# Front of a fused attention and feed-forward kernel: seven sets of six transposes, undivided exponentials, a buffer for each block of words, and second weights loaded by ScalarE

## The chip, the cores and the metric

The kernel runs on one core of a Trainium2 chip. The metric is the device time of one execution in microseconds, and less is better. The core has a matrix engine (TensorE, PE in the rows), VectorE (DVE), ScalarE (ACT), GpSimd (POOL) and a queue engine SyncE (SP) that mostly issues DMA transfers. Each engine works through its own list of instructions in order and waits on semaphores where it needs another's result.

## The reference

```python
w = softmax(weight_gen, axis=-1)            # (4, 4096, 8, 7), float32
x_unf = causal window of 7 rows of x        # x: (4, 4096, 192)
att[b,s,h,g] = sum_k w[b,s,h,k] * x_unf[b,s,k,h,g]     # 8 heads of 24
h = att.reshape(16384, 192) @ w_in          # (192, 2048), float64
g = max(0.01 * h, h)
out = float32(g @ w_out)                    # (2048, 192), float64
```

The inputs w_in and w_out have eight bytes a number; the kernel reads them as pairs of 32-bit words and makes float32 numbers and then two float16 halves of them.

## The kernel before

The 16384 tokens lie on 128 partitions with 128 rows each. A chunk is 4 rows, 512 tokens, and there are 32 chunks. A chunk's attention output is made by thirteen operations on GpSimd (`conv_ops`: one product, then six times product and sum). It is scaled by a power of two per token, split into two float16 halves (`split_h` on ScalarE, `split_l` on GpSimd), transposed by VectorE in blocks (`squares`), written to DRAM (`put_squares`, tile `far`) and read back transposed (`get_squares`, tile `xx`). TensorE then makes for each pair of 128 features the product with w_in (`mm1`, tile `hp`), ScalarE the leaky maximum (`leak`) and the upper half, VectorE the lower half (`gl`), and TensorE the product with w_out (tiles `po`).

The first chunk is another matter, since nothing is loaded or split yet when it starts. Its attention output is made by VectorE and GpSimd together, GpSimd for the last 12 of the 32 groups of a row and head. The sums over the 7 taps are partly left to TensorE: each set of taps is multiplied into a tile `parts`, and TensorE transposes the sets one after the other with `is_transpose`, adding them up in PSUM (`add_transposed`, tile `ta`). Copies then bring the sums to SBUF (`first_tokens`, tile `xw`). Its products run in float32: `mm1(0)` to `mm1(7)`, called product 0 to 7 below, each of six matmuls of 512 columns, and sixteen second products (`mm2_whole`) of four matmuls each.

All of this is written out by hand in the string `START`, a letter for a step. Those which matter here:

- `d`, `g`: the next multiplication (or addition) of a set on VectorE, on GpSimd; `t`: the transposes of the next set; `T`: `first_tokens`; `f`: the next product with its two leaks (`leak_out`) on ScalarE; `e`: the next second product.
- `r`: `read_words`, two ScalarE operations on the next of 16 blocks of words (tiles `rnd` and `mag`); `W` or `w`, `o`: VectorE (or GpSimd) makes float32 numbers of them (`widen`, `round_up`, tile `bits`); `m`: `block_max`, the largest magnitude of a block (tile `most`).
- `1`, `2`, `3`: the scales of the weights. `1` takes the maximum over all 16 block maxima (tile `both`) and has TensorE transpose it into `spares`; VectorE reduces that to `top`, `2` has TensorE spread it, and `3` makes the scales. The float16 halves of the weights come behind it.
- `a`, `b`: softmax of the second half of the first piece of weights; `p`: a GpSimd step of the second chunk's attention; `M`, `N`, `E`, `D`: softmax of the second piece; `B`, `C`, `V`, `y`, `Y`, `X`, `R`: scaling, splitting, transposing, writing and reading back of the second chunk.

Words of w_in come in blocks of 2 x 192 KB (three buffers), those of w_out in blocks of 384 KB (two buffers); all of them are loaded by SyncE, and each `read_words` call asks for a later block. From the second chunk on a loop runs `step(q)` for each pair of features.

Of the kernel before, what the change touches and what calls it, by code (L numbers as in the profile page):

```python
# [8 lines left out]
F32 = mybir.dt.float32  # L9
# [37 lines left out]
SETS = ((6,), (5,), (4, 3), (2,), (1, 0))  # L47
# [19 lines left out]
def conv_attention_moe_kernel(  # L67
# [54 lines left out]
    def load_words(key, eng=nc.sync):  # L122
        q, kind = key
        if kind == IN:
            w = raw.tile([P, NB, P, 2], U32, tag="wi", name="wi_raw", bufs=3)
            for u, r in enumerate(HALVES):
                f = 2 * q + u
                eng.dma_start(out=w[r], in_=w_in_words[:, :, f * P:(f + 1) * P, :])
        else:
            w = raw.tile([P, 2, D, 2], U32, tag="wo", name="wo_raw")  # L130
            eng.dma_start(out=w, in_=w_out_words[:, 2 * q:2 * q + 2, :, :])
        words[key] = w
# [4 lines left out]
    def read_words(key):  # L137
# [3 lines left out]
        nc.scalar.activation(out=rnd, in_=w[:, :, 0], func=AF.Copy, scale=2.0 ** -29)  # L141
        nc.scalar.activation(
            out=mag, in_=w[:, :, 1].bitcast(F32), func=AF.Prelu, scale=REBIAS, alpha=SIGN
        )
        vals[key] = rnd, mag.bitcast(U32)
# [221 lines left out]
    W = J * D + HP  # L367

    def tiles_of_sets():

        tiles = [
            xtp.tile([P, NK, 2, NB, P], F32, tag="parts", name="parts"),
            xtp.tile([P, 2, J, D], F32, tag="sq", name="parts"),
            xtp.tile([P, 2, J, D], F32, tag="split", name="parts"),
        ]
        a, b, c = tiles
        a = a.rearrange("p k i b t -> p (k i b t)")
        b, c = (t.rearrange("p i j d -> p (i j d)") for t in (b, c))
        return [b[:, 0:W], c[:, 0:W], a[:, 0:W], a[:, W:2 * W], a[:, 2 * W:3 * W]]

    def conv_sets(eng, s, w, tmp=None):

        n = s.stop - s.start
        for i, ks in enumerate(SETS):
            dst = parts[i][:, 0:J * D].rearrange("p (h g) -> p h g", g=G)[:, s, :]
            for k in ks:
                out = dst
                if k != ks[0]:
                    t = conv.tile([P, J * D], F32, tag="tmp", name="tmp") if tmp is None else tmp
                    out = t[:, 0:n * G].rearrange("p (h g) -> p h g", g=G)  # L390
                wk = w[:, s, k:k + 1].to_broadcast([P, n, G])
                eng.tensor_tensor(out=out, in0=tap(0, k)[:, s, :], in1=wk, op=ALU.mult)  # L392
                yield
                if k != ks[0]:
                    eng.tensor_tensor(out=dst, in0=dst, in1=out, op=ALU.add)  # L395
                    yield


# [17 lines left out]
    def add_transposed(i):  # L416
# [8 lines left out]
        for b in range(NB):  # L425
            for j in range(J):
                a = (j * NB + b) * HP
                nc.tensor.matmul(
                    out=sums[b][:, j * P:(j + 1) * P], lhsT=v[:, a:a + P],
                    rhs=ident, is_transpose=True, start=(i == 0 and j == 0),  # L430
                    stop=(i == len(SETS) - 1 and j == J - 1), skip_group_check=True,
                )

    def first_tokens():
# [5 lines left out]
        for b in range(NB):  # L440
            h, t = xx[0][:, :, 0, b, :], sums[b].rearrange("p (j t) -> p j t", j=J)
            if b == 0:
                nc.scalar.copy(out=h, in_=t)
            elif b == 1:
                nc.vector.tensor_copy(h, t)
            else:
                nc.scalar.copy(out=h[lo], in_=t[lo])
                nc.vector.tensor_copy(h[hi, 1:J], t[hi, 0:J - 1])
                nc.vector.tensor_copy(h[hi, 0:1], t[hi, J - 1:J])
# [3 lines left out]
    def scale_tokens(c):  # L453

        m = win.tile([P, J, 2], F32, tag="xm", name="xm")[:, :, 0]
# [3 lines left out]
        nc.vector.tensor_reduce(  # L459
            out=m, in_=att[c], axis=AX.X, op=ALU.max, apply_absolute_value=True  # L460
        )
# [3 lines left out]
        nc.gpsimd.tensor_tensor(  # L465
            out=att[c], in0=att[c], in1=up.bitcast(F32).to_broadcast([P, J, D]), op=ALU.mult
        )
# [41 lines left out]
    def mm1(q):  # L509
# [3 lines left out]
        for b in range(NB):  # L513
            b_of = (b, (b + 1) % NB) if c == 0 else (b, b)
            if c < WHOLE:
                w = value((i, IN))
                passes.append(([w[:, k] for k in b_of], xx[c][:, :, 0, b, :]))
                continue
            h, l = xx[c][:, :, 0, b, :], xx[c][:, :, 1, b, :]
            w_h, w_l = ([w[:, i, k] for k in b_of] for w in (wi_h, wi_l))  # L520
# [3 lines left out]
        for m, (w, r) in enumerate(passes):  # L524
            for u, s in enumerate(HALVES):
                nc.tensor.matmul(  # L526
                    out=hp[2 * q + u], lhsT=w[u][s], rhs=r[s],
# [86 lines left out]
    def mm2_whole(ns):  # L614

        for n in ns:
            f = n % NF
            for j in range(J):
                nc.tensor.matmul(  # L619
                    out=po0[j // 2][:, j % 2 * D:(j % 2 + 1) * D],  # L620
                    lhsT=g_h[n][:, j * P:(j + 1) * P], rhs=value((f // 2, OUT))[:, f % 2],
# [82 lines left out]
    def prepare(stage):  # L704
# [9 lines left out]
        if s == "r" and done[s] + 4 <= len(order):  # L714
            load_words(order[done[s] + 3])

    with tc.manual_schedule():
# [44 lines left out]
        def step(q):  # L762
# [18 lines left out]
            else:  # L781
                split_g(2 * q)
                if c == WHOLE and i == TURNS[c][1] + 1:
# [15 lines left out]
            if c + 1 < NCH:  # L799
# [6 lines left out]
                if i == turned:  # L806
                    squares(c + 1, 0)
                    if c != WHOLE:
# [151 lines left out]
```

## Time and profile before

| | us |
|---|---|
| median of 3 runs (lowest, highest) | 1032.48 (1032.46, 1033.61) |
| the profiled execution, its own time | 1032.44 |
| its span, first to last instruction | 1030.7 |
| TensorE busy | 1024.9 |
| GpSimd, ScalarE, VectorE busy | 805.7, 660.2, 566.0 |

The span is what the profile shows in detail; 1.7 us of the profiled execution's time lie around it. Busy time is the time in which an engine had an instruction in work. The page also gives the granted clock of TensorE in forty slices, and it is at its full level in all of them.

### The profile page before, as it was taken

Reading aid. Unit: us, or ns where it says so; the run is one execution under the profiler, and the core shown is the slowest. Engines: PE = TensorE matmul, PEld = TensorE weight load, DVE = VectorE, ACT = ScalarE, POOL = GpSimd, SP = SyncE. Lnnn points to the kernel's source line nnn. Section 1 sums busy time; section 2 is a strip of 40 time slices with the busy share of each in tenths; the row PEclk is TensorE's granted clock in tenths of the full one; section 3 lists DMA queues with packets and bytes.
Section 4 is the critical chain, followed back from the end, with each engine's and each line's share of the span. In section 5 each row is a group of like instructions: output and inputs, shape, how many; then the busy total and the mean of one; then the engine's idle time right before and its main releaser. Section 6 shows DMA issues by size and latency. Waiting matters only on the chain.

```text
span 1030.7 us, 30286 instructions
## 1 busy us (share of the span) xinstructions
PE 1024.9 (99%) x12828; PEld 618.9 (60%) x12828; DVE 566.0 (55%) x1030; ACT 660.2 (64%) x1266; POOL 805.7 (78%) x518
## 2 busy tenths in 40 slices
PE   9999999999999999999999999999999999999998
PEld 7755555565565655555555555565555655656566
DVE  8986555555545555455555555545456454555443
ACT  6576666666666666666666566666666666666664
POOL 7999897777887777987777977778977779977600
PEclk9999999999999999999999999999999999999999
DMA  9432312213223031322213123132320323220120
GB/s 250 147 100 63 126 48 63 95 47 125 55 85 97 32 110 63 110 63 61 94 50 126 48 63 106 36 126 62 94 80 34 109 62 110 63 63 32 48 63 17
DMA packets 42662, 83.08 MB, mean 81 GB/s; under 512 B 4511, under 2 KB 36127, under 8 KB 40734
## 3 DMA queue, kind: packets, MB, share of 16 engines
q1 hardware_dynamic: 42382, 81.05, 25.9%
q8 instruction: 100, 1.64, 0.7%
q14 instruction: 36, 0.29, 0.1%
q10 hardware_dynamic: 144, 0.10, 0.0%
HBM read 56.36 MB, written 24.77 MB: 79 GB/s over the span
## 4 chain that ended last, share of the span: by engine, by line
PE 97%; DMA 1%; POOL 1%; DVE 1%; ACT 0%; issue 0%; SPq 0%; DVEq 0%; POOLq 0%
PE hp L526 49%; PE po L579 47%; PE po L619 1%; DMA xx<-far 0%; POOL parts L392 0%; DVE sq L484 0%; DMA far<-sq 0%; DMA wt<-in_weight_gen_dram 0%; POOL parts L395 0%; POOL tmp L392 0%; DVE gl L550 0%; SPq L501 0%; ACT wt L324 0%; DVE gh L549 0%; ACT hp L532 0%
## 5 line engine op out<-in xcount | busy, mean ns | idle before, releaser
L550 DVE TENSOR_TENSOR gl<-hp,gh 128x512 f16<-128x512 f32 x496 | 335.9, 687 | 345.3 <-ACT gh L547 344.1
L579 PE MATMUL po<-wo,gh 64*128 64x384 f16 (+1 forms) x4096 | 506.5, 318 | 0.0
L579 PE MATMUL po<-wo,gl 64*128 64x192 f16 x3968 | 486.4, 243 | 0.4 <-DVE gl L550 0.3
L532 ACT ACTIVATE hp<-hp 128x512 f32<-128x512 f32 x496 | 292.3, 589 | 274.2 <-PE hp L526 274.1
L526 PE MATMUL hp<-xx,wi_h 64*128 64x512 f16 x2976 | 443.3, 376 | 0.4 <-DMA xx<-far 0.4
L364 POOL TENSOR_TENSOR acc<-acc,tmp 128x768 f32<-128x768 f32 x186 | 336.5, 1809 | 14.6
L547 ACT CAST gh<-hp 128x512 f16<-128x512 f32 x495 | 290.7, 587 | 15.8 <-PE po L579 1.3
L360 POOL TENSOR_TENSOR tmp<-xt,wt 128x768 f32<-128x768 f32 x186 | 287.8, 1547 | 10.0
L526 PE MATMUL hp<-xx,wi_l 64*128 64x512 f16 x1488 | 282.8, 376 | 0.0
L579 PEld LDWEIGHTS <-gh 64*128 64x128 f16 x4096 | 198.4, 94 | 138.9
L526 PEld LDWEIGHTS <-wi_h 64*128 64x128 f16 x2976 | 141.3, 94 | 135.0 <-DMA xx<-far 1.1
L579 PEld LDWEIGHTS <-gl 64*128 64x128 f16 x3968 | 193.0, 94 | 29.8 <-DVE gl L550 1.3
L465 POOL TENSOR_TENSOR acc<-acc,xu 128x768 f32<-128x768 f32 x31 | 45.5, 1469 | 137.2 <-DVE xu L202 137.2
L526 PEld LDWEIGHTS <-wi_l 64*128 64x128 f16 x1488 | 72.7, 94 | 88.2
L484 DVE STREAM_TRANSPOSE sq<-split 128x384 f16<-128x384 f16 x124 | 63.8, 554 | 51.0 <-POOL split L475 50.6
L662 DVE SCALAR_TENSOR_TENSOR ot<-po,xr,ot 128x192 f32<-128x192 f32 x120 | 41.8, 411 | 47.9 <-ACT ot L658 47.9
L471 ACT CAST split<-acc 128x768 f16<-128x768 f32 x31 | 25.8, 832 | 51.0 <-POOL acc L465 51.0
L475 POOL TENSOR_TENSOR split<-acc,split 128x768 f16<-128x768 f32 x31 | 50.9, 1642 | 1.9 <-ACT split L471 1.9
L360 POOL TENSOR_TENSOR acc<-xt,wt 128x768 f32<-128x768 f32 x31 | 48.1, 1552 | 0.2
L658 ACT ACTIVATE ot<-po,xr 128x192 f32<-128x192 f32 x120 | 40.7, 422 | 0.0
L459 DVE TENSOR_REDUCE xm<-acc 128x4 f32<-128x768 f32 x31 | 29.2, 943 | 2.4 <-POOL acc L364 2.4
L619 PE MATMUL po<-bits,g 128*128 128x192 f32 x128 | 22.3, 330 | 0.0
(85 smaller groups left out, 289.7 us busy)
## 6 DMA issues: line engine op xcount, KB each, us to landing
xx<-far SPq DMA_DIRECT2D x124, 192.0 KB, 3.7
xt<-in_x_dram SPq DMA_DIRECT2D x14, 1344.0 KB, 5.8
far<-sq SPq DMA_DIRECT2D x31, 384.0 KB, 2.3
out_dram<-ot SPq DMA_DIRECT2D x62, 192.0 KB, 1.9
wt<-in_weight_gen_dram SPq DMA_DIRECT2D x15, 224.0 KB, 2.6
wi_raw<-in_moe_w_in_dram SPq DMA_DIRECT2D x16, 192.0 KB, 6.2
wo_raw<-in_moe_w_out_dram SPq DMA_DIRECT2D x8, 384.0 KB, 5.4
xt<-in_x_dram SPq DMA_DIRECT2D x2, 384.0 KB, 4.2
```

What stands on the lines that cost most here:

```text
L360: eng.tensor_tensor(out=out, in0=tap(c, k), in1=wk, op=ALU.mult)
L364: eng.tensor_tensor(out=acc, in0=acc, in1=out, op=ALU.add)
L465: nc.gpsimd.tensor_tensor(out=att[c], in0=att[c], in1=up.bitcast(F32).to_broadcast([P, J, D]), op=ALU.mult)
L475: eng.tensor_tensor(out=l, in0=att.pop(c), in1=h, op=ALU.subtract)
L484: nc.vector.transpose(out=sq[c][:, v, i], in_=src[:, v])
L526: nc.tensor.matmul(out=hp[2 * q + u], lhsT=w[u][s], rhs=r[s], start=(m == 0), stop=(m == len(passes) - 1),)
L532: return nc.scalar.activation(out=hp[n], in_=hp[n], func=AF.Prelu, alpha=0.01, scale=DOWN).ins
L547: nc.scalar.copy(out=h, in_=t)
L550: nc.vector.tensor_tensor(out=l, in0=t, in1=h, op=ALU.subtract)
L579: ins = nc.tensor.matmul(out=po[j][:, 0:b - a], lhsT=g[n][s, j * P:(j + 1) * P], rhs=wo[s, f, a:b], start=(f == 0 and i < HALF and m == 0) ...
L658: nc.scalar.activation(out=ot[:, j], in_=po[k * HALF + j][:, D:2 * D], func=AF.Copy, scale=rx[j])
L662: nc.vector.scalar_tensor_tensor(out=ot[:, j], in0=po[k * HALF + j][:, 0:D], scalar=rx[j], in1=ot[:, j], op0=ALU.mult, op1=ALU.add,)
```

## The change

The sets of taps become seven, one for each tap, so that no additions stand on VectorE or GpSimd; each set is transposed in six blocks of 128 columns instead of twelve overlapping ones, which drops the small ScalarE copy ahead of each set. The sums of the six blocks lie in two PSUM tiles, and `first_tokens` copies them to places of their own by eight copies, four on ScalarE and four on VectorE; `first_rows` says where each product finds its halves, and `POS` in which order the second product takes the tokens.

The second half of the first piece keeps its exponentials undivided; the sums are taken by `s` and their reciprocals go into the scaling of the second chunk (`by_head`). Each block of words has a buffer of its own, so SyncE asks for all of w_in at once in step `A`, with the second piece's weights and rows behind it. ScalarE asks for the first four blocks of w_out behind its first exponential (`<`) and for one more at each `z`. `read_words` does `mag` before `rnd`. Last, `squares(c + 1, 1)` of the later chunks moves one step later.

```diff
-SETS = ((6,), (5,), (4, 3), (2,), (1, 0))
+TURNED = (0, 3, 1, 4, 2, 5)
+POS = (0, 2, 1, 3)
 START = (
-    "ZASgdddgtggddtddrgdggtdggrttaWwoTbrrpWrpWf"
-    "rWmppf"
-    "rWrWmpf"
-    "rWmrWmmKppeeeerWmprWmkppf"
-    "rWmrWmMppf"
-    "rWmrWmpWmpNeeeef"
-    "EBCVmmmmf"
-    "e1De2eyY3Xevvhhllevvhhlle"
-    "RvvhhllfvvhhllqqHL"
+    "ZA<Sgdgdtgdtgdrtgdtagdtgdttwbo"
+    "TcrpmWp"
+    "rmfW"
+    "rpWmzrfWm"
+    "rpWmzrsf"
+    "WmzrpWmpeeeerWmf"
+    "rpWmzrWmMppf"
+    "rWmrWmpppprWmNeeeef"
+    "BErWmrWmCVmf"
+    "1eDe2eyY3XevvhhlleRvvhhllevvhhllfvvhhllqqHL"
 )
-            w = raw.tile([P, NB, P, 2], U32, tag="wi", name="wi_raw", bufs=3)
+            w = raw.tile([P, NB, P, 2], U32, tag="wi", name="wi_raw", bufs=NQ)
...
+            w = raw.tile([P, 2, D, 2], U32, tag="wo", name="wo_raw", bufs=NQ)
...
-        v = parts[i]
-        nc.scalar.copy(out=v[:, J * D:W], in_=v[:, 0:HP])
-        for b in range(NB):
-            for j in range(J):
-                a = (j * NB + b) * HP
-                nc.tensor.matmul(
...
+        for n, m in enumerate(TURNED):
+            nc.tensor.matmul(
+                out=sums[n // J][:, n % J * P:(n % J + 1) * P],
+                lhsT=parts[i][:, m * P:(m + 1) * P], rhs=ident, is_transpose=True,
...
+        act(out=x[:, 1:3], in_=a)
+        dve(x[lo, 3], a[hi, 1])
+        dve(x[hi, 0], a[lo, 0])
+        act(out=x[:, 5], in_=b)
+        dve(x[lo, 0], a[hi, 0])
+        dve(x[hi, 3], b[lo])
+        act(out=x[hi, 4], in_=a[lo, 1])
+        act(out=x[lo, 4], in_=b[hi])
...
-                if c == WHOLE and i == TURNS[c][1] + 1:
+                if c + 1 < NCH and i == TURNS.get(c, (1, 3))[1] + 1:
                     squares(c + 1, 1)
...
-        if s == "r" and done[s] + 4 <= len(order):
-            load_words(order[done[s] + 3])
...
+            elif what == "<":
+                for q in range(NQ // 2):
+                    load_words((q, OUT), nc.scalar)
+            elif what == "z":
+                load_words((NQ // 2 + sent, OUT), nc.scalar)
+                sent += 1
```

How instructions stand is shown at three places. The first is ScalarE around the leaks of product 5, the first `g<-hp` row of each piece. `rnd` and `mag` are the two halves of `read_words`, `wt<-wt` the exponential of the second piece, `split` the upper half of the second chunk. Before:

```order
L141 ACTIVATE rnd<-wo_raw 128x384
L142 ACTIVATE mag<-wo_raw 128x384
L141 ACTIVATE rnd<-wo_raw 128x384
L142 ACTIVATE mag<-wo_raw 128x384
L537 ACTIVATE g<-hp 128x512 x2
L324 ACTIVATE wt<-wt 128x448
L471 CAST split<-acc 128x768
L537 ACTIVATE g<-hp 128x512 x2
```

and now:

```order
L557 ACTIVATE g<-hp 128x512 x2
L327 ACTIVATE wt<-wt 128x448
L144 ACTIVATE mag<-wo_raw 128x384
L147 ACTIVATE rnd<-wo_raw 128x384
L144 ACTIVATE mag<-wo_raw 128x384
L147 ACTIVATE rnd<-wo_raw 128x384
L493 CAST split<-acc 128x768
L557 ACTIVATE g<-hp 128x512 x2
```

The last two blocks of words were read ahead of the leaks of product 5 and are now read behind them and behind the exponential.

The second place is TensorE from products 5 and 6 (the row of twelve matmuls into `hp`) to the two steps of the scales (`spares`); a second product is four matmuls into `po`. Before:

```order
L526 MATMUL hp<-xw,bits 128x512 x12
L619 MATMUL po_114<-bits,g 128x192 x2
L619 MATMUL po_115<-bits,g 128x192 x2
L215 MATMUL spares<-ident,both 1x128 x2
L619 MATMUL po_114<-bits,g 128x192 x2
L619 MATMUL po_115<-bits,g 128x192 x2
L223 MATMUL spares<-top,ones 128x2
```

and now:

```order
L546 MATMUL hp<-xw,bits 128x512 x12
L218 MATMUL spares<-ident,both 1x128 x2
L639 MATMUL po_114<-bits,g 128x192 x2
L639 MATMUL po_115<-bits,g 128x192 x2
L639 MATMUL po_114<-bits,g 128x192 x2
L639 MATMUL po_115<-bits,g 128x192 x2
L226 MATMUL spares<-top,ones 128x2
```

The transposes of `both` stood behind one second product and now stand right behind product 6.

The third place is VectorE from its first multiplication of the first chunk (`parts<-xt,po_114`) to the copies of the first tokens (`xw<-ta`). `mx<-wt` is the maximum over the second half of the weights, which needs the second load of `wt`. Before:

```order
L392 TENSOR_TENSOR parts<-xt,po_114 128x480 x3
L392 TENSOR_TENSOR spares<-xt,po_114 128x480
L395 TENSOR_TENSOR parts<-parts,spares 128x480
L392 TENSOR_TENSOR parts<-xt,po_114 128x480 x2
L392 TENSOR_TENSOR spares<-xt,po_114 128x480
L395 TENSOR_TENSOR parts<-parts,spares 128x480
L316 TENSOR_REDUCE mx<-wt 128x32
L152 TENSOR_SCALAR po_115<-mag 128x384
```

and now:

```order
L386 TENSOR_TENSOR parts<-xt,po_114 128x480 x5
L319 TENSOR_REDUCE mx<-wt 128x32
L386 TENSOR_TENSOR parts<-xt,po_114 128x480 x2
L155 TENSOR_SCALAR bits<-mag 128x384
L434 COPY xw<-ta 64x256
L435 COPY xw<-ta 64x256
L437 COPY xw<-ta 64x256
L438 COPY xw<-ta 64x256
```

The maximum stood behind all multiplications and now stands ahead of the last two.

## Rows read from the trace of the kernel before

**Rows 1.** The page's first part: busy time, share of the span, instructions.

```profile
PE 1024.9 (99%) x12828; PEld 618.9 (60%) x12828; DVE 566.0 (55%) x1030; ACT 660.2 (64%) x1266; POOL 805.7 (78%) x518
```

**Rows 2.** Waits of PE: who for whom, total us, times, longest.

```profile
PE hp L526 <- DMA xx<-far: 0.4, 1, 0.4
PE po L579 <- DVE gl L550: 0.3, 1, 0.3
```

**Rows 3.** Timeline of PE: start, length, instruction, count, idle before and its end.

```profile
6.75 6.74 PE L428 MATMUL ta<-ident,parts 128*128 128x128 f32 x60
13.58 8.00 PE L526 MATMUL hp<-xw,bits 64*128 64x512 f32 x36
...
43.00 1.57 PE L619 MATMUL po<-bits,g 128*128 128x192 f32 x8
44.40 0.38 PE L215 MATMUL spares<-ident,both 128*1 128x128 f32 x2
...
54.40 0.38 PE L526 MATMUL hp<-xx,wi_h 64*128 64x512 f16 x1
55.14 0.60 PE L526 MATMUL hp<-xx,wi_h 64*128 64x512 f16 x3 [0.36 <-DMA xx<-far]
```

**Rows 4.** Line 428 on PE: length min/median/max in ns, first and last start.

```profile
L428 PE MATMUL ta<-ident,parts x60: 272/273/298, 6.8 to 13.2; 128*128 128x128 f32 x60
```

**Rows 5.** Timeline of DVE and ACT, 6 to 15 us.

```profile
6.32 1.22 DVE L392 TENSOR_TENSOR parts<-xt,po 128x480 f32<-128x480 f32 x2 [0.16 <-DMA xt<-in_x_dram]
...
11.11 0.38 DVE L316 TENSOR_REDUCE mx<-wt 128x32 f32<-128x224 f32 x1
...
12.66 0.39 ACT L324 ACTIVATE wt<-wt 128x224 f32<-128x224 f32 x1 [1.01 <-POOL wt L319]
...
12.96 0.57 ACT L443 COPY xw<-ta 128x512 f32<-128x512 f32 x1
...
14.14 0.56 DVE L448 COPY xw<-ta 64x384 f32<-64x384 f32 x1 [0.36 <-ACT xw L447]
```

**Rows 6.** Line 284, second load of `wt`: its issue, and us to landing.

```profile
L284 SPq DMA_DIRECT2D wt<-in_weight_gen_dram x1: 598/598/598, 4.7 to 4.7; - x1
...
DMA to landing us min/median/max: 3.7/3.7/3.7
```

**Rows 7.** Busy time by stretch; last three: granted PE clock, DMA share, GB/s.

```profile
1.00:2.00 1.00, 0.54 (x1) 0.50 (x2) 0.54 (x3) 1.00 (x1) 0.29 (x1) 1.00 0.14 25
...
5.00:9.00 4.00, 4.00 (x26) 3.46 (x25) 3.73 (x8) 1.33 (x4) 3.57 (x6) 1.00 1.10 261
```

**Rows 8.** Timeline of ACT, 36 to 42 us.

```profile
36.30 0.54 ACT L142 ACTIVATE mag<-wo_raw 128x384 f32<-128x384 f32 x1
40.52 1.09 ACT L537 ACTIVATE g<-hp 128x512 f32<-128x512 f32 x2 [3.68 <-PE hp L526]
41.50 0.58 ACT L324 ACTIVATE wt<-wt 128x448 f32<-128x448 f32 x1
```

**Rows 9.** Timeline of DVE and POOL, 36 to 45 us.

```profile
36.89 0.55 DVE L152 TENSOR_SCALAR spares<-mag 128x384 uint32<-128x384 uint32 x1
37.47 0.56 DVE L157 CUSTOM_DVE_ANT_0 bits<-spares,rnd 128x768 uint16<-128x768 uint16 x1
37.95 0.54 DVE L185 TENSOR_REDUCE most<-bits 128x1 f32<-128x384 f32 x1
39.23 0.96 POOL L319 TENSOR_TENSOR wt<-wt,mx 128x448 f32<-128x448 f32 x1
...
40.78 1.92 DVE L185 TENSOR_REDUCE most<-bits 128x1 f32<-128x384 f32 x4
42.74 0.17 DVE L212 TENSOR_REDUCE both<-most 128x2 f32<-128x16 f32 x1
...
43.74 0.56 DVE L899 RECIPROCAL sm<-spares 128x64 f32<-128x64 f32 x1
...
44.82 0.41 DVE L221 TENSOR_REDUCE top<-spares 1x2 f32<-1x256 f32 x1 [0.52 <-PE spares L215]
```

More of the change, by code (lines that the diff above doesn't have):

```diff
@@ L144, in read_words @@
         )
+        nc.scalar.activation(out=rnd, in_=w[:, :, 0], func=AF.Copy, scale=2.0 ** -29)
         vals[key] = rnd, mag.bitcast(U32)
@@ L365, in conv_ops, with conv_sets @@
             yield
-    W = J * D + HP
+    NM = J * D // P
     def tiles_of_sets():
         tiles = [
-            xtp.tile([P, NK, 2, NB, P], F32, tag="parts", name="parts"),
             xtp.tile([P, 2, J, D], F32, tag="sq", name="parts"),
             xtp.tile([P, 2, J, D], F32, tag="split", name="parts"),
-        ]
[L376 to L381, printed above, removed]
-        n = s.stop - s.start
[L384 to L396, printed above, removed]
+            xtp.tile([P, 2, J, D], F32, tag="xx", name="parts", bufs=2),
+            xtp.tile([P, 2, J, D], F32, tag="xx", name="parts", bufs=2),
+        ]
+        return [t[:, m].rearrange("p j d -> p (j d)") for t in tiles for m in range(2)]
+    def conv_sets(eng, s, w):
+        n = s.stop - s.start
+        for i, k in enumerate(reversed(range(K))):
+            eng.tensor_tensor(
+                out=parts[i].rearrange("p (h g) -> p h g", g=G)[:, s, :], in0=tap(0, k)[:, s, :],
+                in1=w[:, s, k:k + 1].to_broadcast([P, n, G]), op=ALU.mult,
+            )
+            yield
     def run(ops, n=None):
@@ L420, in add_transposed @@
         if i == 0:
-            for b in range(NB):
+            for b in range(2):
                 sums.append(ps_h.tile([P, TOK], F32, tag="h", name="ta"))
-        v = parts[i]
-        nc.scalar.copy(out=v[:, J * D:W], in_=v[:, 0:HP])
-        for b in range(NB):
-            for j in range(J):
-                a = (j * NB + b) * HP
-                nc.tensor.matmul(
[L429 to L432, printed above, removed]
+        for n, m in enumerate(TURNED):
+            nc.tensor.matmul(
+                out=sums[n // J][:, n % J * P:(n % J + 1) * P],
+                lhsT=parts[i][:, m * P:(m + 1) * P], rhs=ident, is_transpose=True,
+                start=(i == 0 and n % J == 0), stop=(i == K - 1 and n in (J - 1, NM - 1)),
+                skip_group_check=True,
+            )
     def first_tokens():
@@ L439, in first_tokens, with first_rows @@
         lo, hi = HALVES
[L440 to L449, printed above, removed]
+        x = xx[0].rearrange("p k i b t -> p (k i b t)").rearrange("p (n t) -> p n t", t=2 * P)
+        a = sums[0].rearrange("p (n t) -> p n t", n=2)
+        b = sums[1][:, 0:2 * P]
+        act, dve = nc.scalar.copy, nc.vector.tensor_copy
+        act(out=x[:, 1:3], in_=a)
[6 more added lines that the diff above has]
+        act(out=x[lo, 4], in_=b[hi])
+    def first_rows(b):
+        x = xx[0].rearrange("p k i b t -> p (k i b t)").rearrange("p (n t) -> p n t", t=2 * P)
+        return [x[s, n:n + d + 1:d] for s, (n, d) in zip(HALVES, PAIRS[b])]
+    PAIRS = (((1, 2), (0, 2)), ((0, 5), (1, 2)), ((2, 2), (4, 1)))
     split, sq, undo_of, downs = {}, {}, {}, {}
     def scale_tokens(c):
+        by_head = c == WHOLE
         m = win.tile([P, J, 2], F32, tag="xm", name="xm")[:, :, 0]
```

80 lines of the change are left out of this document (49 added, 31 removed).

## Prediction

> **What bounds the kernel now.** The busy times come first: TensorE 99% of the span, the others 55 to 78% [rows 1]. The waits of TensorE say how full that is: behind its start it waits 0.4 us for `xx` and 0.3 us for `gl` [rows 2]. The timeline of TensorE shows where work and waits lie: sixty transposes from 6.75 us, product 0 at 13.58, then no gap until 54.78 (54.40 + 0.38), then 0.36 us of waiting for the second chunk's `xx`, and the second chunk from 55.14 [rows 3]. So the kernel is TensorE's list, laid end to end from 13.58 us. The change keeps every matmul behind that point. It can move the time in two ways: where the list starts, and which waits it opens before the second chunk. I work out both, as the time at which the second chunk starts, against 55.14 us. The profiled execution took 1032.44 us with a span of 1030.7; the median of the runs shown is 1032.48, so sums against the execution hold for the median.
>
> **The transposes.** Sixty start between 6.8 and 13.2 us, 0.109 us apart without a hole [rows 4]: TensorE itself sets the start of product 0. Eighteen fewer save 18 x 0.109 = 1.96 us, and the last would end at 13.49 - 1.96 = 11.53 us. The last six then hold the first PSUM tile until t = 11.3 (two transposes earlier). VectorE keeps pace as long as nothing else holds it: two multiplications take 1.22 us [rows 5], so from 6.32 six of them and the maximum (0.38) end at about 10.4.
>
> **The load of the second weights.** The maximum now stands ahead of the last two multiplications, so VectorE waits in front of them for the second load of `wt`. It was issued at 4.7 and landed 3.7 us later, at 8.4 [rows 6], and nobody noticed, since the maximum came at 11.11 [rows 5]. Now ScalarE's first three loads of w_out (1152 KB) go out behind its first exponential, and their data move from about 5.3 us: the exponential ends at 4.1, and between SyncE's first issue at 0.75 and the first traffic, late in the stretch of 1 to 2 us, lies about 1.1 us [rows 7]. From 5 to 9 us the DMA engines are full, share 1.10 at 261 GB/s [rows 7], so these bytes take another's turn. SyncE's queue had about 2.7 us of transfers ahead of the landing at 8.4 when they begin (the rest of the rows `xt`, which end VectorE's wait at 6.32, then 384 KB of w_in and `wt`). If the queues share evenly, that part takes twice as long: `wt` lands at 11.1. Lower bound: no loss, 8.4. Upper bound: ScalarE's 1152 KB go first, 4.5 us at 261 GB/s, 12.9. I take 11.1, since full engines leave no room for none. The maximum and two multiplications then end at 11.1 + 0.4 + 1.2 = 12.7, and t = 13.35 (four transposes of 0.109, and 0.27 for the last to end).
>
> The Trainium skill says the same in "DMA: Bandwidth & Descriptors", section "Issuing engines are not separate DMA queues": transfers issued by different engines run on the same 16 DMA engines and interleave, and a second issuing engine saves issue time alone. It speaks against this part of the change: by it `wt` comes at about 11.1, without it at 8.4. The full share in the rows agrees; no row of before has two queues at once.
>
> **The first tokens.** One ScalarE copy of 512 columns takes 0.57 and one VectorE copy of 64x384 takes 0.56 [rows 5]; the new VectorE copies of 64x256 I estimate at 0.42, 0.35 apart. In the old row VectorE waited 0.36 us for ScalarE's copy out of the same tile [rows 5], so I let the two engines take turns on a tile: ScalarE's first copy ends at t + 0.57, VectorE's four end at t + 2.05, ScalarE's last at t + 2.5. Product 0 starts at about t + 1.1. Behind ScalarE's last copy stand the exponential (0.39) and the two reads of block 1, and VectorE's addition behind these (0.47 from one read to the next, 0.57, 0.56): product 1 can start at t + 4.5. Product 0 would be done at t + 3.75, so TensorE waits 0.75 us again. In the kernel before product 1 came at 13.58 + 8.00/3 = 16.25 [rows 3]. With t = 13.35 it comes at 17.85, which is 1.6 us later; with t = 11.3 at 15.8, 0.45 earlier.
>
> **The scales.** This is the dearest term, and it does not depend on the start. Let X be the time at which ScalarE begins the leaks of product 5: it had waited 3.68 us for TensorE there, and X was 40.52 [rows 8]. TensorE reached the end of product 6 at 43.00 [rows 3], X + 2.48. The last two blocks of words are now read behind X. ScalarE: leaks and exponential to X + 1.5 (the exponential began at X + 0.98 and the next can start 0.5 later), four reads 0.47 apart, so `mag` and `rnd` of block 14 end at X + 2.0 and X + 2.5, those of block 15 at X + 3.0 and X + 3.5 [rows 8]. VectorE: shift of block 14 from X + 2.07, addition 0.58 later, its maximum 0.48 behind, the next shift 0.46 behind that, and again, then the one maximum still open, 0.48 each, and `both` (0.17) [rows 9]: 2.07 + 0.58 + 0.48 + 0.46 + 0.58 + 0.48 + 0.48 + 0.74 = X + 5.87. TensorE can start the transposes of `both` at X + 5.93, so it stands idle for 5.93 - 2.48 = 3.45 us. Before, `both` was done at 42.91 and TensorE came at 44.40, after one second product: no wait [rows 3, 9]. Bounds: if each ScalarE and VectorE step costs 0.05 us less 2.9, if 0.05 more 4.0.
>
> Two chains lead from there to the second chunk. TensorE's own work between 43.00 and 54.78 is unchanged, 11.78 us, so it arrives at 54.78 + 3.45. The other runs through `top`, the block transposes and two DMA transfers: from `top` at 44.82 [rows 9] to 55.14 are 10.3 us. VectorE's three softmax operations ended 1.39 us behind `both`; now `top` stands behind them at X + 5.87 + 1.39 = 47.8, and `xx` comes at 58.1. The chains arrive together, 58.2 and 58.1, and the old wait of 0.36 is used up.
>
> **Parts at nothing.** Undivided exponentials take one GpSimd operation out and put four small operations into VectorE's scaling of the second chunk. GpSimd's attention of that chunk still ends about 39, at the softmax step that began at 39.23 [rows 9], and the scaling, about 2.1 us, is done by 41.4, ahead of X + 2.07 = 42.6. If contention moved the chunk's rows by more than 1 us it would show here. The moved `squares` work on VectorE (55% busy [rows 1]), some steps ahead of the chunk's use; TensorE's whole wait for VectorE's `gl` is 0.3 us [rows 2], so neither gain nor loss is there to be had.
>
> **Sum.** Scales +3.45, start +1.6, old wait -0.36: 4.7 us, 1032.44 + 4.7 = 1037.1. With the other bounds of the load: 8.4 gives 3.45 - 0.45 - 0.36 = +2.6 (1035.1); 12.9 gives +6.5 (1038.9).
>
> **Rivals.**
> *No contention.* The loads of w_out slip in between: 1035.1, from the lower bound. For it: no row shows two queues sharing, so the even split is an assumption. Against it: the full DMA share.
> *The whole saving passed on.* All 1.96 us of the eighteen transposes reach product 1, because copies and reads overlap better than my turns: 3.45 - 1.96 - 0.36 = +1.1, 1033.6, no difference that can be told (0.2%, or 2.1 us, is about what can be told here). It decides as soon as product 1 comes 1.0 us earlier than before. For it: the transposes without a hole. Against it: exponential and reads stand behind the copies on ScalarE.
> *No wait at the scales.* If TensorE did not stand in front of `both`, the start alone would decide, and with the whole saving the time would be 1032.44 - 1.96 - 0.36 = 1030.1. Against it: the order, in which TensorE and ScalarE both depend on product 5.
> *The clock.* The granted clock is 1.00 throughout [rows 7]. TensorE never stood idle for 3 us behind its start; if the clock fell from 2.4 to 1.2 GHz there, two second products (2 x 1.4 us) at half speed would add 2.8 us, 1039.9, and all work up to the second chunk 11.8 us. The Trainium skill, "TensorE: Matmul & The Clock Gate", Part 1, says that an idle TensorE is put back to the lower level and that activity releases it; no row of before shows a fall.
>
> **How the numbers follow.** Shared load with the wait at the scales 50% (own range 1036.0 to 1038.9), no contention 20%, whole saving 12%, clock 12%, no wait at the scales 6%. Predicted is the first, 1037.1. The range of 1033.4 to 1040.0 reaches from just under the whole saving to just over the fall of the clock; it leaves out the last rival, the long fall, and edges, some 15%. Slower by over 0.2%: the first, the clock and most of no contention, 80%. Within 0.2%: the whole saving and the rest of no contention, 14%. Faster: 6%.
>
> **What would show it.** Transposes x42 with a hole in front of the last twelve and VectorE's `mx` waiting for the load of `wt` at about 11 us; product 1 behind a wait, near 17.9; above all a wait of TensorE of about 3.5 us for `both` in front of the transposes into `spares`, near 48; the second chunk near 59.8. The prediction is wrong if `wt` lands before 9, if TensorE's wait for `both` is under 2 us, or if the second chunk starts earlier than 57.

## The result, and the profile after

The changed kernel takes 1039.97 us (median of five executions, 1037.17 to 1041.14), against 1032.46 before on the same chip. The ratio is 1.0069, with an interval of 1.0052 to 1.0085: slower. The forecast was 1037.1 in a range of 1033.4 to 1040.0. The median is 2.9 us above the forecast and 0.03 us below the upper end of the range; two of the five executions lie above it.

The profiled execution is the fastest of the five: 1037.17 us, span 1035.2, mean granted clock 1.000. The other four show a mean clock of 0.994 to 0.998. So the profile is to be held against the steps of the prediction, and the other four need an explanation of their own. First the page's busy times, and the waits of TensorE:

```profile
PE 1023.3 (99%) x12810; PEld 618.0 (60%) x12810; DVE 568.0 (55%) x1032; ACT 658.5 (64%) x1263; POOL 803.6 (78%) x515
```

```profile
PE spares L218 <- DVE both L215: 3.5, 1, 3.5
PE ta L416 <- DVE parts L386: 1.8, 1, 1.8
...
PE hp L546 <- DVE xw L434: 1.0, 1, 1.0
PE hp L546 <- DVE bits L160: 0.5, 1, 0.5
```

TensorE has 1.6 us less work than in [rows 1], and where [rows 2] had 0.4 and 0.3 us of waiting there are now 6.8. The timeline of TensorE shows where:

```profile
6.34 3.73 PE L416 MATMUL ta<-ident,parts 128*128 128x128 f32 x30
11.85 1.53 PE L416 MATMUL ta<-ident,parts 128*128 128x128 f32 x12 [1.77 <-DVE parts L386]
14.39 3.26 PE L546 MATMUL hp<-xw,bits 64*128 64x512 f32 x12 [1.01 <-DVE xw L434]
18.17 5.42 PE L546 MATMUL hp<-xw,bits 64*128 64x512 f32 x24 [0.52 <-DVE bits L160]
...
48.61 0.38 PE L218 MATMUL spares<-ident,both 128*1 128x128 f32 x2 [3.53 <-DVE both L215]
48.83 2.77 PE L639 MATMUL po<-bits,g 128*128 128x192 f32 x16
...
59.91 1.01 PE L546 MATMUL hp<-xx,wi_h 64*128 64x512 f16 x4
```

Against [rows 3]: the transposes now have a hole in front of the last twelve, product 1 starts at 18.17 (16.25 before), a wait of 3.53 us stands in front of the transposes of `both`, and the second chunk starts at 59.91 without a wait for `xx` (55.14 before, behind one). That is 4.77 us, and the execution is 4.73 us longer. The hole is VectorE's, which waits for the second weights; its timeline from 6 to 12 us, and the line that loads `wt`:

```profile
6.52 2.35 DVE L386 TENSOR_TENSOR parts<-xt,po 128x480 f32<-128x480 f32 x4 [0.49 <-DMA xt<-in_x_dram]
10.85 0.39 DVE L319 TENSOR_REDUCE mx<-wt 128x32 f32<-128x224 f32 x1 [1.98 <-DMA wt<-in_weight_gen_dram]
11.15 1.21 DVE L386 TENSOR_TENSOR parts<-xt,po 128x480 f32<-128x480 f32 x2
```

```profile
L287 SPq DMA_DIRECT2D wt<-in_weight_gen_dram x2: 380/488/597, 0.7 to 4.6; - x2
...
DMA to landing us min/median/max: 2.0/4.1/6.3
```

The load issued at 4.6 took 6.3 us, where [rows 6] had 3.7. The long wait is at the scales. ScalarE and then VectorE from 31 us, to be read against [rows 8, 9]:

```profile
31.79 0.60 ACT L557 ACTIVATE g<-hp 128x512 f32<-128x512 f32 x1 [4.47 <-PE hp L546]
...
42.54 1.08 ACT L557 ACTIVATE g<-hp 128x512 f32<-128x512 f32 x2 [4.21 <-PE hp L546]
43.51 0.58 ACT L327 ACTIVATE wt<-wt 128x448 f32<-128x448 f32 x1
43.98 0.55 ACT L144 ACTIVATE mag<-wo_raw 128x384 f32<-128x384 f32 x1
...
45.30 0.54 ACT L147 ACTIVATE rnd<-wo_raw 128x384 uint32<-128x384 uint32 x1
```

```profile
33.35 0.56 DVE L155 TENSOR_SCALAR spares<-mag 128x384 uint32<-128x384 uint32 x1 [2.11 <-ACT mag L144]
...
41.99 0.95 DVE L462 TENSOR_REDUCE spares<-acc 128x32 f32<-128x768 f32 x1
...
44.56 0.56 DVE L155 TENSOR_SCALAR spares<-mag 128x384 uint32<-128x384 uint32 x1 [0.32 <-ACT mag L144]
45.26 0.56 DVE L160 CUSTOM_DVE_ANT_0 bits<-spares,rnd 128x768 uint16<-128x768 uint16 x1
...
48.39 0.17 DVE L215 TENSOR_REDUCE both<-most 128x2 f32<-128x16 f32 x1
```

With X = 42.54, `both` starts at X + 5.85 and its transposes at X + 6.07; the forecast was 5.93. But the row at 44.56 also says that VectorE waited only 0.32 us for `mag` of block 14 (blocks count from 0). Until 44.24 (X + 1.70) it had been at work without a wait of note since 33.35: first on blocks 9 to 13, then on the scaling of the second chunk, which begins at 41.99. And at 33.35 it had waited 2.11 us for block 9, which ScalarE reads behind the leaks of product 3 (at 31.79). The kernel before reads 12, 14 and 16 blocks ahead of the leaks of products 3, 4 and 5, the changed kernel 9, 11 and 14.

### The profile page after: what moved, and what is told of

The parts are those of the page before. It is cut to its first block, busy times and chain, and to the rows that moved or that the text cites. A ratio compares the mean times of both kernels' runs of the same rounds, so it can differ in the third digit from the quotient of the medians.

```text
span 1035.2 us, 30244 instructions
## 1 busy us (share of the span) xinstructions
PE 1023.3 (99%) x12810; PEld 618.0 (60%) x12810; DVE 568.0 (55%) x1032; ACT 658.5 (64%) x1263; POOL 803.6 (78%) x515
## 3 DMA queue, kind: packets, MB, share of 16 engines
q8 instruction: 100, 1.64, 0.7%
## 4 chain that ended last, share of the span: by engine, by line
PE 97%; DVE 1%; DMA 1%; ACT 0%; issue 0%; SPq 0%; DVEq 0%; ACTq 0%
PE hp L546 48%; PE po L599 47%; PE po L639 2%; DMA wt<-in_weight_gen_dram 1%; DVE bits L160 0%; DVE spares L155 0%; DVE most L188 0%; PE ta L416 0%; SPq L131 0%; ACT mag L144 0%; ACT wt L327 0%; DVE mx L319 0%; ACT g L557 0%; ACT xw L433 0%; DVE parts L386 0%
## 5 line engine op out<-in xcount | busy, mean ns | idle before, releaser
L546 PE MATMUL hp<-xw,bits 64*128 64x512 f32 x96 | 22.4, 600 | 1.5 <-DVE xw L434 1.0
```

Source lines behind the costliest of these rows:

```text
L546: nc.tensor.matmul(out=hp[2 * q + u], lhsT=w[s], rhs=r[u], start=(m == 0), stop=(m == len(passes) - 1),)
```

## The experiments

The transposes, the loads, the place of the reads and the clock are taken apart one by one. Ratios are to the kernel before on the same chip. All edits but one are to the changed kernel.

**The same kernel again**, to see in a trace what a longer execution does.

> The changed kernel as it is, to catch in a trace what lifts its median 2.8 us over its profiled execution (1037.17 us, granted clock 1.000; the other four executions 1039.6 to 1041.1 at a mean clock of 0.994 to 0.998). Theory A (the wait at the scales): the granted clock falls behind TensorE's wait of 3.53 us for `both`, so in an execution of about 1040 us the second products and the first matmuls behind 48.6 us stand at twice their length, and what lies ahead of 48 us is as in the execution of 1037.17. Theory B (the start): it falls behind the holes of 1.77 and 1.01 us ahead of product 0, and product 0 or 1 is stretched; the second chunk then starts later than 59.91 although the wait for `both` is still about 3.5. Rival C: it falls somewhere in the later chunks, and the second chunk starts at 59.9 whatever the time. An execution near 1037 with a clock of 1.000 tells nothing of this.

Measured: 1039.56 us (1037.28 to 1041.02, four executions), ratio 1.006 [1.0046, 1.0074]. The profiled execution took 1041.02 at a mean clock of 0.995. Its timeline of TensorE, and its windows (columns as in [rows 7]; the third figure from the end is the granted clock):

```profile
15.31 10.92 PE L546 MATMUL hp<-xw,bits 64*128 64x512 f32 x36 [0.83 <-DVE xw L434]
26.16 5.47 PE L639 MATMUL po<-bits,g 128*128 128x192 f32 x32
...
51.26 0.38 PE L218 MATMUL spares<-ident,both 128*1 128x128 f32 x2 [3.54 <-DVE both L215]
51.48 4.45 PE L639 MATMUL po<-bits,g 128*128 128x192 f32 x16
...
64.24 0.60 PE L546 MATMUL hp<-xx,wi_h 64*128 64x512 f16 x4
```

```profile
10.00:12.00 2.00, 0.72 (x7) 0.48 (x5) 0.23 (x1) 0.81 (x2) 0.31 (x1) 1.00 1.11 310
...
16.00:18.00 2.00, 2.00 (x6) 1.56 (x6) 1.36 (x4) 1.81 (x5) 0.65 (x1) 0.50 1.12 225
...
52.00:54.00 2.00, 2.00 (x8) 2.00 (x8) 1.97 (x6) 0.00 (x0) 1.24 (x2) 0.50 0.04 8
```

Theories A and B both hold: the granted clock stood at its lower level (0.50, 1.2 GHz) in two places, from about 14 to 21 us behind the holes of the start, and from about 51.5 to 55 us behind the wait for `both`. The second chunk starts 4.33 us later than at full clock, which splits into three: product 0 starts 0.92 later (15.31 for 14.39), products 0 and 1 with their wait take 10.85 instead of 9.13 (26.16 - 15.31 and 23.52 - 14.39), +1.72, and from the transposes of `both` to those of `top` 4.60 us pass instead of 2.91 (51.26 to 55.86, and 48.61 to 51.52), +1.69. The whole execution is 3.85 longer. The 0.92 was in neither theory.

**The loads of w_out later.**

```diff
-    "ZA<Sgdgdtgdtgdrtgdtagdtgdttwbo"
+    "ZASgdgdtgdtgdr<tgdtagdtgdttwbo"
```

> ScalarE asks for the first four blocks of w_out behind its first read of words, no longer behind its first exponential. Theory (shared DMA engines): the second load of `wt` lands near 8.4 instead of 10.82, VectorE's maximum no longer waits 1.98 us, the last twelve transposes follow without the 1.77 us hole, and product 1 starts about 1.9 us earlier than 18.17; the wait for `both` stays at 3.5 and the second chunk starts near 58.0, so the time is about 1.9 us under that of the changed kernel at the same clock. Rival (the load of `wt` is late for another reason, SyncE's own queue): landing and hole stay, the time too. Second rival (the words decide): the start gains 1.9 us, but the blocks of words, which ScalarE and VectorE work off one by one, don't come earlier, and the wait for `both` grows by what the start gained.

Measured: 1037.11 us (1036.90 to 1037.24), ratio 1.0038 [1.0026, 1.0051], 2.45 us under the changed kernel on the same chip. TensorE:

```profile
6.75 4.95 PE L416 MATMUL ta<-ident,parts 128*128 128x128 f32 x42
...
16.49 5.42 PE L546 MATMUL hp<-xw,bits 64*128 64x512 f32 x24 [0.53 <-DVE bits L160]
...
46.94 0.38 PE L218 MATMUL spares<-ident,both 128*1 128x128 f32 x2 [3.52 <-DVE both L215]
47.15 4.39 PE L639 MATMUL po<-bits,g 128*128 128x192 f32 x16
...
59.87 0.60 PE L546 MATMUL hp<-xx,wi_h 64*128 64x512 f16 x4
```

The hole is gone, `wt` landed 3.7 us after its issue as before, and product 1 starts 1.68 earlier. The wait for `both` is the same to 0.01 us, so it does not depend on the start. Here all five executions have a mean clock of 0.998, and this trace shows where it goes: the second products behind the wait take 4.39 us for 2.77. Without this fall (1.62) the second chunk would stand at 58.25, near the 58.0 expected. Also, the five executions lie within 0.34 us, where the changed kernel's lie within 4.

**The reads earlier.**

```diff
-    "WmzrpWmpeeeerWmf"
-    "rpWmzrWmMppf"
-    "rWmrWmpppprWmNeeeef"
-    "BErWmrWmCVmf"
+    "WmzrpWmpeeeerWmzrWmrWmf"
+    "rpWmrWmMppf"
+    "rWmpppprWmrWmNeeeef"
+    "BECVmf"
```

> The last two blocks of words are read ahead of the leaks of product 5 again, as in the kernel before, and one block more ahead of those of product 4; nothing else is changed. Theory (the place of the two reads makes the wait at the scales): ScalarE reads them in its waits for TensorE, `both` is ready at about X + 2.4 as before, TensorE's wait for `both` falls from 3.53 to under 0.6 us and the second chunk starts near 57.0, with the time about 3 us lower. Rival (the words as a whole are late): VectorE needs about 1.7 us for each of the 16 blocks and is behind by itself, so `both` comes at most 1 us earlier wherever ScalarE reads, TensorE's wait stays above 2.5 us and the time falls by under 1 us. If the clock falls because of this wait, its mean should be nearer to 1.000 by the first theory and unchanged by the rival.

Measured: 1037.10 us (1036.04 to 1037.56), ratio 1.0036 [1.0024, 1.0049]. TensorE, then VectorE's first operation of the second chunk's scaling:

```profile
18.88 5.42 PE L546 MATMUL hp<-xw,bits 64*128 64x512 f32 x24 [0.53 <-DVE bits L160]
...
47.26 0.38 PE L218 MATMUL spares<-ident,both 128*1 128x128 f32 x2 [1.47 <-DVE both L215]
...
59.91 0.60 PE L546 MATMUL hp<-xx,wi_h 64*128 64x512 f16 x3 [0.97 <-DMA xx<-far]
```

```profile
44.29 0.95 DVE L462 TENSOR_REDUCE spares<-acc 128x32 f32<-128x768 f32 x1
```

The edit does more than its text says: 11, 13 and 16 blocks are now read ahead of the leaks of products 3, 4 and 5, where the changed kernel has 9, 11 and 14. The wait falls by 2.06 us, and VectorE's timeline says why: the wait of 2.11 us for block 9 is gone, and the one of 0.32 for block 14. So most of the gain comes from the reads ahead of product 3's leaks; the last two by themselves could hardly have given more than 0.32 us in this kernel (an estimate from VectorE's rows above; it was not run). The rest of the wait stays because VectorE now comes to the scaling and to `both` only behind all words, and with the scaling late at 44.29 `xx` is late too: 0.97 us of the gain turns into a wait for `xx`, and from product 1 to the second chunk it is 41.03 us instead of 41.74. Neither theory had this third outcome, though the rival was right that VectorE is behind by itself: in this trace it works without a wait from 21.77 us to `both`. Three of the five executions have a clock of 1.000.

**One second product ahead of `both`.**

```diff
-    "1eDe2eyY3XevvhhlleRvvhhllevvhhllfvvhhllqqHL"
+    "e1eDe2yY3XevvhhlleRvvhhllevvhhllfvvhhllqqHL"
```

> One second product (1.4 us) is put ahead of the transposes of `both`, where the kernel before has it; it is taken from behind them, so TensorE's work is the same. Theory (TensorE's idle time is the loss): the wait for `both` falls from 3.53 to about 2.1 us, but `xx`, which hangs on `both` through VectorE and two transfers, comes no earlier than before, and the forecast had it level with TensorE, so the second chunk starts within 0.3 us of 59.91 and the time at a clock of 1.000 stays at 1037; with no single idle stretch over 2.2 us the clock stays at 1.000 in most executions and the median falls from 1040 to about 1037. Rival 1 (TensorE alone decides): `xx` has room, the second chunk starts 1.4 us earlier and the time falls by 1.4 us more. Rival 2 (the clock falls at the start or later): the median stays near 1040.

Measured: 1038.86 us (1037.51 to 1039.62), ratio 1.0053 [1.0039, 1.0067]. The wait for `both` was 2.04 us, and 1.43 us of waiting for `xx` came back in front of the second chunk, 42.26 us behind product 1 (41.74 in the changed kernel). So filling the wait with work taken from behind it wins nothing there: `xx` hangs on VectorE, as the theory said. The other half of the theory fell: the median did not come down to 1037. In this trace the clock was at 1.00 behind `both` but at 0.50 from 13 to 16 us, behind the holes of the start, which this edit leaves.

**One queue.** SyncE asks for all words in the order of use; `<` and the `z` are gone.

```diff
-                for q in range(2, NQ):
-                    load_words((q, IN))
+                for key in order[2:14]:
+                    load_words(key)
                 load_weights(1)
+                for key in order[14:]:
+                    load_words(key)
                 load_rows(1)
```

> All blocks of words are asked for by SyncE again, w_in and w_out in the order in which they are read, each still with a buffer of its own; ScalarE asks for none of them. The reads stay where the changed kernel has them. Theory (two things stand apart: the loads make the start late, the place of the two reads makes the wait at the scales): no hole ahead of the last twelve transposes, product 1 near 16.5 as with the later loads, a wait for `both` of about 3.5 as there, the clock falling behind it, and so about 1037 us with a clock of 0.998. Rival (the words): with one queue the blocks of w_out come in time for every read, the words don't fall behind, and the wait for `both` is under 2.5 us, the time under 1036.

Measured: 1036.53 us (1036.20 to 1037.65), ratio 1.0039 [1.0027, 1.0052]. Product 1 at 16.67; and

```profile
47.12 0.58 PE L218 MATMUL spares<-ident,both 128*1 128x128 f32 x2 [3.52 <-DVE both L215]
```

the same wait. The rival falls: words that come in order do not shorten it. VectorE waits 2.94 us for block 9 here and 0.31 for block 14, so the reads hold it at the same two places.

**The wait filled**, in the kernel with the later loads.

```diff
-    "1eDe2eyY3XevvhhlleRvvhhllevvhhllfvvhhllqqHL"
+    "jj1eDe2eyY3XevvhhlleRvvhhllevvhhllfvvhhllqqHL"
+            elif what == "j":
+                heat(4)
```

> The kernel with the later loads (loads_late) and eight more matmuls of zeros, 0.42 us each, on TensorE between product 6 and the transposes of `both`; their results are used by nothing, and nothing waits for them but TensorE's own list. In loads_late the two second products behind the wait of 3.52 us took 4.39 us instead of 2.77 at a granted clock of 0.53 to 0.62. Theory (TensorE's idle time makes the clock fall): with the stretch filled the clock stays at 1.00, the second products take 2.77 us, the second chunk starts 1.6 us earlier than 59.87, and the median is near 1035.5 (1037.1 less 1.6). Rival (it falls for something else, such as the length of the execution so far or the load on the other engines): the time stays at 1037.1 with a clock of 0.998.

Measured: 1035.98 us (1034.53 to 1036.74, six executions), all at a clock of 1.000; ratio 1.0031 [1.0019, 1.0042].

```profile
42.97 2.11 PE L856 MATMUL heat<-zeros 128*128 128x512 f32 x8
46.57 0.38 PE L218 MATMUL spares<-ident,both 128*1 128x128 f32 x2 [1.49 <-DVE both L215]
46.78 2.77 PE L639 MATMUL po<-bits,g 128*128 128x192 f32 x16
```

The fills took 0.26 us each, not 0.42, so 1.49 us stayed idle, and still the second products took 2.77 us. From product 1 to the second chunk it is 41.74 us (16.12 to 57.86) instead of 43.38: the 1.64 us of the theory. In this stretch TensorE got faster by doing more. In the whole time the gain is less sure: the medians are from two chips, and the intervals of the two ratios overlap.

**The kernel before with late reads.**

```diff
-    "rWmrWmpWmpNeeeef"
-    "EBCVmmmmf"
+    "WmmmmmppNeeeef"
+    "BErWmrWmCVf"
```

> The kernel before with one part of the change alone: the last two blocks of words are read behind the leaks of product 5 and behind the exponential instead of ahead of them, and the scaling of the second chunk stands ahead of their additions on VectorE; the maxima still open are taken before. The start, the loads and everything else are of before, with one second product ahead of the transposes of `both`. Theory (the place of the reads alone makes the wait): `both` is ready at about X + 5.4 = 45.9 instead of 42.91, TensorE comes at 44.40 and waits about 1.5 to 2 us, and the chain through `top` and the two transfers puts the second chunk at about 57.6, 2.5 us later than before, so about 1035 us. Rival (the wait in the changed kernel comes from words that are late as a whole): here the words are in time, `both` is late by less than 1 us, and the time stays within 1 us of 1032.5.

Measured: 1035.62 us (1035.41 to 1036.25, six executions), ratio 1.0031 [1.0019, 1.0042]: 3.2 us for this one part.

```profile
46.66 0.38 PE L215 MATMUL spares<-ident,both 128*1 128x128 f32 x2 [2.07 <-DVE both L212]
...
58.52 0.60 PE L526 MATMUL hp<-xx,wi_h 64*128 64x512 f16 x3 [1.44 <-DMA xx<-far]
```

```profile
43.01 0.56 DVE L152 TENSOR_SCALAR spares<-mag 128x384 uint32<-128x384 uint32 x1 [2.19 <-ACT mag L142]
```

The part alone opens the wait, since here VectorE is not behind and waits 2.19 us for `mag` of block 14. TensorE's wait is 2.07 us behind a second product of 1.4, some 3.5 in all. `xx` is 0.9 us later than forecast.

**The start filled, and both.**

```diff
-    "ZA<Sgdgdtgdtgdrtgdtagdtgdttwbo"
+    "ZA<Sgdgdtgdtgdrtgdtagdtgdjttwbo"
+            elif what == "j":
+                heat(6)
```

Both kernels keep the tile of the first `heat` for this; the second adds the fill of the wait.

> The changed kernel with six more matmuls of zeros (0.26 us each, as the fill took in fill_wait) on TensorE ahead of the last twelve transposes, where it waits 1.8 to 2.3 us for VectorE. They may take longer than the hole by a little, and nothing else waits for them. Theory (the idle stretches at the start make the clock fall in those executions in which it falls ahead of 25 us): products 0 and 1 run at the full clock in every execution, the times above 1039 are gone, and what is left above 1037.2 is the fall behind the wait for `both`, at most 1.7 us: median 1037 to 1038.9. Rival (the fall at the start comes from something else, such as the copies' wait of 1.0 us that stays): the executions reach from 1037 to 1041 as before.

> The changed kernel with both fills: six matmuls of zeros ahead of the last twelve transposes and eight ahead of the transposes of `both`. Theory (the clock alone lifts the median over the forecast): the granted clock is 1.000 in all executions, the second chunk starts near 59.9 as in the execution of 1037.17, and the median is 1037.2, within 0.7 us, that is 2.4 to 2.8 us under the unfilled kernel though TensorE has more work. Rival (the load of `wt` lands at other times in other executions and that alone spreads the times): the median stays near 1039.6 with a clock of 1.000.

Measured: with the start filled 1038.41 us (1037.32 to 1040.63), ratio 1.0054 [1.0042, 1.0067]; the trace shows products 0 and 1 at full clock, 0.50 behind `both` and 4.45 us for its second products. One execution of five still stood above 1039, against the theory. With both filled 1038.68 us (1038.10 to 1039.34), ratio 1.0056 [1.0043, 1.0069], and clocks of 0.999 to 1.000. So the clock is not all: at full clock these five still lie 1 to 2 us above 1037.2. VectorE's timeline shows why, to be read against the same two rows of the changed kernel:

```profile
7.59 2.35 DVE L386 TENSOR_TENSOR parts<-xt,po 128x480 f32<-128x480 f32 x4 [1.37 <-DMA xt<-in_x_dram]
12.49 0.39 DVE L319 TENSOR_REDUCE mx<-wt 128x32 f32<-128x224 f32 x1 [2.55 <-DMA wt<-in_weight_gen_dram]
```

The first rows came 1.07 us later than in the execution of 1037.17, `wt` 1.64 later (7.7 us after its issue), product 1 started at 19.82 and the second chunk at 61.56, each 1.65 later. In the trace of 1041.02 `wt` took 7.1 us. The rival of this expectation is right in part: the landing itself moves from execution to execution. For the first rows that needs no second queue: in one_queue they came at 7.01, in `ordered` at 6.27.

**Both repairs together.**

> Both single repairs together: ScalarE asks for the first blocks of w_out behind its first read (as in loads_late) and the last three blocks are read ahead of the leaks of products 4 and 5 (as in reads_early). Theory (two separate parts that add up): product 1 near 16.5 as in loads_late; from product 1 to the second chunk 41.0 us as in reads_early, with a wait for `both` of about 1.5 and one for `xx` of about 1.0; second chunk near 57.5, clock at 1.000, about 1034.8 us. Rival (the wait for `both` that is left in reads_early, 1.47 us, is there because words come late by the loads): it grows by what the start gains, to over 2.5 us, and the time stays above 1036.

Measured: 1035.99 us (1035.89 to 1037.89), ratio 1.0037 [1.0023, 1.0051].

```profile
45.95 0.38 PE L218 MATMUL spares<-ident,both 128*1 128x128 f32 x2 [1.98 <-DVE both L215]
46.16 4.38 PE L639 MATMUL po<-bits,g 128*128 128x192 f32 x16
```

Between the two theories: the wait is 1.98, and earlier in this trace ScalarE waited 1.61, 0.98 and 0.73 us for blocks of w_in to land, so words do come late here. The clock fell behind the wait, but this execution was no longer than the three at 1.000 (1035.89 to 1036.03), so the fall seems to have cost what a wait for `xx` would have; that is argued, not shown.

**A version from the findings** (`ordered`). Loads as in `one_queue`, `rnd` first again, and

```diff
-    "ZASgdgdtgdtgdrtgdtagdtgdttwbo"
-    "TcrpmWp"
+    "ZASgdgdtgdtgdrtgdtagdtgdttwbor"
+    "TWcprmWp"
...
-    "WmrpWmpeeeerWmf"
+    "WmrpWmpeeeerWmrWmrWmf"
...
-    "rWmrWmpppprWmNeeeef"
-    "BErWmrWmCVmf"
+    "rWmpppprWmNeeeef"
+    "BECVmmf"
```

> A version made from the findings: the seven sets, eight copies and undivided exponentials of the change, but all words asked for by SyncE in the order of use, block 1 read and added ahead of the first tokens' copies, all other blocks read ahead of the leaks of product 5, and the scaled words ahead of `mag` in each read as before. Theory: no hole ahead of the last transposes, product 1 right behind product 0 at about 15.4 (before 16.25), `both` in time so that TensorE waits under 0.5 us, and the second chunk near 54.3, which is 0.9 us earlier than before: about 1031.6 us with a clock of 1.000, faster than both kernels by a little. Rival (VectorE or the attention of the second chunk on GpSimd is the next bound): a wait for `both` or `xx` of over 1 us stays, and the time is 1032.5 or more.

Measured: 1030.98 us (1030.48 to 1032.55, eleven executions, all at 1.000), ratio 0.9988 [0.9979, 0.9997]: a little faster than before, and by the two ratios some 8 us faster than the changed kernel.

```profile
12.14 8.41 PE L546 MATMUL hp<-xw,bits 64*128 64x512 f32 x36 [1.01 <-DVE xw L434]
...
41.98 0.38 PE L218 MATMUL spares<-ident,both 128*1 128x128 f32 x2
...
53.27 0.60 PE L546 MATMUL hp<-xx,wi_h 64*128 64x512 f16 x4
```

From 12.14 us on the list of TensorE's waits has none, and the second chunk starts 1.87 us earlier than in [rows 3].

> The version `ordered` with `mag` ahead of `rnd` in each read, as in the change. In the rows VectorE's addition follows the shift 0.69 us later with `mag` first and 0.58 to 0.60 with `rnd` first. Theory (the addition then needs a wait of its own for `rnd`, 0.1 us on VectorE for each of fifteen blocks): VectorE falls behind by up to 1.6 us until `both`, where it had no room to speak of, so a wait for `both` of 0.3 to 0.8 us opens and the time is that much over `ordered`, 1031.3 to 1031.8. Rival (the shift can start earlier by one ScalarE step with `mag` first, which gives back the 0.1 us): no wait, the same time within 0.2 us.

Measured: 1031.80 us (1031.64 to 1033.91, eleven executions), ratio 0.9996 [0.9987, 1.0005]. VectorE reached the scaling 26.33 us behind product 0, 0.91 later than in `ordered` (25.42), where the theory had up to 1.6; but no wait for `both` opened, 0.57 us for `xx` did. The two intervals overlap, and in the two traces the transposes start 0.57 apart as well (6.74 and 6.17), so that the whole 0.8 us come from `mag` is not shown.

## Why the prediction was right and where it was wrong

*The transposes and the load.* Right. Forty-two transposes, a hole before the last twelve, `wt` landing at 10.8 (11.1 forecast), t near 13.2 (13.35). The cause is shown by loads_late and one_queue: with ScalarE's loads away from the start `wt` landed 3.7 and 4.5 us behind its issue and the hole before the last twelve closed. That the even split came so near is luck in part, since over the six traces with ScalarE's early loads VectorE's maximum starts anywhere from 10.85 to 12.49. The Trainium skill, "DMA: Bandwidth & Descriptors", section "Issuing engines are not separate DMA queues", says that transfers of several issuing engines interleave on the same 16 engines; these runs agree: 6.2 to 7.7 us from issue to landing with ScalarE's loads asked for ahead of it, 3.7 to 4.5 without.

*The first tokens.* Product 1 came 0.3 us late though t was 0.2 early, so the chain from t took 5.0 us for 4.5: VectorE's copies started 0.45 apart, not 0.35, and its addition 0.69 behind the shift, not 0.58.

*The scales.* The size is right to 0.1 us (3.53 for 3.45), the account only in part. ScalarE's chain behind X ran as forecast, and the kernel before with late reads shows that the place of the last two reads can open the wait by itself (3.2 us). But the change also moved reads behind the leaks of products 3 and 4, which the forecast passed over, and VectorE waits there (2.11 us). The forecast had the scaling done at 41.4, X + 0.9; it was done at X + 1.70, only 0.32 us before `mag` of block 14. So two chains of nearly one length lead to `both`, and that the one in the forecast ended last is luck in part. Moving the reads up at all three places took 2.06 us off the wait; what the last two alone are worth in the changed kernel was not run. The old wait for `xx` was used up, as forecast.

*The parts at nothing* showed no wait of their own in TensorE's list; they were not tried singly.

*The sum.* 1037.1 against 1037.17 for an execution at full clock. Two small errors cancel in it: product 1 was 0.3 later than forecast, and the stretch from there to the second chunk grew by 2.85 us (41.74 for 38.89), not by 3.09. The median is another matter. The step that failed is in how the numbers follow: the fall of the clock was given 12% as a rival, when seven of nine executions of the changed kernel show a mean clock under 1.000, and its price was put at 2.8 us for the second products, where the fall behind the wait cost 1.7. It fell at the start as well, for another 1.7 in the traced execution, which the forecast did not have. And `wt` and the first rows were given one landing time each (11.1, and VectorE "from 6.32"), where they moved by 1.6 and 1.1 us between the changed kernel's first trace and that with both fills. The median stayed inside the range by 0.03 us, and four of the nine executions lie above it: that is luck. How the 2.9 us of the median divide between clock and landing stays open: only two executions of this kernel have a trace, one with neither, one with 0.92 of landing and 3.41 of clock. The mean clock alone does not settle it: two executions at 0.998 took 1038.55 and 1039.97.

The Trainium skill, "TensorE: Matmul & The Clock Gate", Part 1, says that activity releases the lower clock and idleness brings it back. The filled wait agrees (six executions at 1.000, where five unfilled ones had 0.998). But the profiled execution of the changed kernel waited 3.53 us and kept 1.00, and waits of 2.04 us (one second product ahead) and 1.98 us (both repairs) were followed by 1.00 and by 0.50. What decides it is open.

## What to carry to other kernels

A wait is priced in two coins where one engine is the bound: its length, and the clock behind it; a profile of one execution at full clock can hide the second, so compare its clock with the other executions'. Ask of an early load what else is on the transfer engines, and of a read whether it stands behind the product that its consumer ends on; then follow the engine that works on what was read, since its own backlog can end at the same time. Filling an engine's idle stretch with useless work can pay, but here moving the producers was worth more (`ordered`).

## What the runs showed that was not expected

With `mag` ahead of `rnd` VectorE's addition starts 0.70 us behind the shift (44.56 to 45.26), where it was 0.58 with `rnd` first [rows 9]. The shift needs `mag` alone, and the addition both; with `mag` first it needs a wait of its own for `rnd`, which fits the 0.1 us a block. Eight matmuls of zeros took 2.11 us in the filled wait, 0.26 each, where the first twelve of the program take 4.4 to 5.5 us, 0.36 to 0.46 each, though the granted clock is 1.00 there too [rows 7]; why is open.
